# A fused attention and two-layer kernel: GpSimd takes norms, sums of v and low halves for all units, and the opening has a new order

## The chip, the core and the metric

The kernel runs on one core of a Trainium2 chip. The metric is the device time of one execution in microseconds. Five engines work side by side: TensorE (PE; its weight loads, PEld, overlap its products), VectorE (DVE), ScalarE (ACT), GpSimd (POOL) and SyncE (SP), which here only issues DMAs.

## The reference

Three stages follow each other. Attention on q, k, v of 4 x 8 heads, 576 positions and 64 columns is a sum of two parts: one over means of four neighbouring positions, repeated four times, and one local, over the positions at a distance below 4. Then come two feed-forward layers, the first without a nonlinearity other than a product.

```python
q_d, k_d, v_d = (means over 4 positions)
out_up = np.repeat(sm_attn(q_d, k_d, v_d), 4, axis=2)
scores = np.where(np.abs(pos[:, None] - pos[None, :]) < 4, scale * q @ k.T, -1e9)
x = out_up + softmax(scores) @ v                  # (2304, 512)
x = ((x @ w1) * (x @ w2)) @ w3 @ w_out            # d_ff 1024
h = x @ w_in; return (h * sigmoid(h)) @ w_out2    # d_ff 2048
```

## The kernel before

The heads are worked in 16 units of two heads (unit u is batch u // 4, pair u % 4). The two matrices w3 and w_out of the first layer are multiplied with each other once (64 products of weights, a PSUM bank of 128x512 each), so that one product is left behind a * b. All inputs are 64-bit floats; a weight arrives as pairs of 32-bit words, and four steps turn them into a 32-bit float: a scale on ScalarE (L210) and shift, clamp and join on VectorE (L221, L215, L227). Operands of the large products are split into a high half (ScalarE) and a low half (a subtraction), and three passes are summed.

The program has an opening, a middle and an end. The opening is written out by hand: `OPENING` is a list of step names, and every engine runs the steps that concern it in the order of that list, so the list sets the order on TensorE, VectorE, ScalarE, GpSimd and the DMA queue of SyncE at once. An engine that waits for one step holds up all of its later ones. After the list the same kinds of steps for units 7 to 15 are placed between products by a table of due times.

Names in the list, with the unit's number at the end: `Lq`, `Lr`, `Lva`, `Lvb` load q and k, v in groups of four, and v in windows; `pq` sums q and k over four positions (VectorE); `s` and `sd` are the scores, local and coarse; `mk`, `ml`, `md` mask and maxima; `x0` to `x2` and `xd` the exponentials with their sums; `rl` and `rd` inverses of the sums; **`n0` to `n2` and `nd` the norms** (exponentials times inverse); `tl0` to `tl2`, `td0`, `td1` transposes of the result on TensorE, `cl`, `cd` their copies out of PSUM; **`pv0`, `pv1` the sums of v**; `od`, `ol` the products with v; `os`, `xf` the sum x, `xh` its high half, **`xo` its low half**. `L` with `wt`, `wo`, `ww12_` loads a weight, `a`, `d2`, `d1`, `d3` are the four decode steps (scale, shift, clamp, join), `h`, `l` the halves of a w12 piece. `p` with half, group and number is one product of weights; `z0`, `z1` are wide products on zeros that only keep TensorE at work, as the nine at the very start do. `ab`, `af`, `cf`, `Sc` are products with w1 and w2, copy, product a * b and store; the first twelve groups of them stand in the list.

Before the change a unit's number decides on the engine: for units 0 to 4 the norms are twelve ScalarE instructions, and `pv` and `xo` run on VectorE; from unit 5 on all three run on GpSimd, a norm as one instruction over all blocks, issued by the step `n0` (`n1`, `n2` do nothing then). `Ed` is the tile of coarse exponentials, `band` that of local ones, `vr` and `vd` those of v.

Of the kernel before, what the change touches and what calls it, by code (L numbers as in the profile page):

```python
# [11 lines left out]
ALU = mybir.AluOpType  # L12
# [6 lines left out]
NQB, QW, KW = 9, 32, 38  # L19
# [27 lines left out]

OPENING = """
Lwt000 Lwt001 Lwt002 Lq0 Lwo00 Lwo01 Lwt010 Lwt011 at00a d2t00a Lwo10 d1t00a Lwo11 at00b d3t00a
d2t00b d1t00b d3t00b Lva0 at00c d2t00c d1t00c d3t00c Lvb0 s0 pq0 Lr0 ao0a d2o0a sd0 z0 z1 mk0 ml0  # L50
Lq1 ao0b d1o0a d3o0a x00 md0 p000 Lwo20 x10 d1o0b p001 d2o0b xd0 d3o0b Lq2 p002 d2t01 x20 p003 rd0
Lwo21 at01 rl0 p004 p005 nd0 d1t01 Lwt020 p006 d3t01 Lwt021 n00 Lwo30 td00 n10 d2o1 td10 Lwo31 p007
n20 pv00 ao1 pv10 Lwt030 pq1 s1 cd00 cd10 tl00 tl10 d1o1 Lr1 cl00 sd1 cl10 d3o1 tl20 od0 Lwt031 cl20
md1 p010 os0 xd1 pq2 p011 Lq3 ao2 p012 d2o2 Lwt100 p013 rd1 mk1 nd1 p014 d1o2 Lwt101 d3o2 sd2 at02
d2t02 s2 Lww12_00 md2 p015 d1t02 p016 Lww12_01 d3t02 ao3 p017 ml1 ol0 Lq4 d1o3 x01 Lwt110 p020 pv01
x11 pv11 p021 d2o3 Lva1 x21 d3o3 p022 at03 p023 rl1 Lr2 d2t03 p024 n01 d1t03 n11 p025 d3t03 Lvb1 n21
p026 pq3 p027 Lwt111 p030 d2t10 at10 xf00 p031 Lww12_20 xf10 xh00 td01 d1t10 xh10 td11 cd01 d3t10
Lww12_21 p032 cd11 xd2 tl01 d2w12_0 tl11 p033 xo00 cl01 rd2 cl11 tl21 xo10 aw12_0 p034 mk2 ml2 od1
cl21 wh00 d1w12_0 p035 nd2 p036 os1 wh01 d3w12_0 p037 x02 ol1 wh02 wh03 pv02 p100 x12 Lva2 Lvb2 p101
x22 xf01 p102 xf11 hw12_0 rl2 td02 pv12 td12 n02 d2t11 Lr3 p103 n12 lw12_0 p104 n22 d2w12_2 sd3 xh01  # L60
xh11 xo01 cd02 s3 xo11 cd12 md3 tl02 at11 Lq5 tl12 pq4 p105 cl02 p106 cl12 aw12_2 d1t11 tl22 d3t11
od2 cl22 xd3 p107 os2 Lwt120 d1w12_2 p110 Lwt121 d3w12_2 sd4 rd3 ol2 Lww12_30 hw12_2 mk3 Lww12_31
ml3 nd3 p111 lw12_2 Lva3 Lvb3 x03 p112 xf02 p113 x13 xf12 pv03 td03 x23 d2t12 td13 p114 pv13 at12
md4 Lr4 p115 rl3 xh02 d1t12 s4 xh12 n03 d3t12 p116 Lq6 n13 p117 xo02 Lwt130 n23 xo12 Lwt131 p120
d2w12_3 cd03 cd13 pq5 p121 xd4 tl03 tl13 pv04 aw12_3 p122 rd4 p123 cl03 d1w12_3 cl13 nd4 tl23
d3w12_3 od3 p124 cl23 os3 Lww12_10 hw12_3 mk4 p125 Lww12_11 ml4 at13 p126 lw12_3 p127 x04 d1t13 ol3
x14 d2t13 d3t13 x24 sd5 Lva4 Lvb4 pv14 s5 Lww12_50 rl4 Lr5 xf03 aw12_1 p131 md5 pq6 xh03 Lww12_51
p130 p134 p133 n14 xo03 p135 p137 wh10 xf13 td04 td14 n04 Lq7 ab000a d2w12_1 cd04 cd14 p132 d1w12_1
tl04 xd5 n24 d3w12_1 od4 ab000b s6 ab000c p136 cl04 os4 tl14 wh11 wh13 ab001a ab001b Lr6 tl24 af00
wh12 ab001c ab100a Lq8 cl14 d2w12_5 mk5 xh13 Lva5 ml5 Lww12_40 ab101a cl24 cf00 ol4 xo13 ab020a  # L70
aw12_5 rd5 pv05 x25 x15 ab021a Lww12_41 xf14 Sc00 Lvb5 ab020b xf04 d1w12_5 ab100b nd5 ab100c x05
af10 td05 ab101b ab101c rl5 hw12_1 td15 d3w12_5 ab020c xh04 cf10 ab030a ab030b Lva6 cd15 Lww12_60
ab021b n05 ab021c n15 n25 cd05 pv15 tl05 lw12_1 xo04 tl15 af02 cl05 ab030c af03 ab031a ab031b ab031c
cl15 Lr7 sd6 Sc10 pv06 hw12_5 ab120a tl25 cf02 d2w12_4 Sc02 Lww12_61 cf03 md6 aw12_4 Sc03 xd6 ab121a
ab110a pq7 ab120b cl25 xh14 ab121b ab130a ab130b mk6 od5 pv16 s7 ab110b ab110c ml6 x26 os5 pv07 x06
ab120c d1w12_4 ab121c ol5 d3w12_4 af12 ab130c ab111a Lq9 af11 rd6 x16 cf12 af13 hw12_4 ab111b xo14
nd6 ab011a lw12_5 ab111c ab010a xf05 ab010b ab011b aw12_6 rl6 ab131a ab010c cf11 n06 td06 xf15 Lr9
ab131b n16 n26 tl06 af01 Lww12_70 Lww12_71 cd06 Lva8 ab050a cl06 Sc12 xh15 tl16 d2w12_6 ab011c
lw12_4 Lvb8 d1w12_6 cf01 tl26 mk7 ml7 ab131c cf13 ab050b cl16 td16 cl26 sd7 xh05 ab150a cd16 xo05
od6 ab150b ab150c aw12_7 ab050c Lvb6 ab051a ab051b md7 ab051c ab151a xd7 pq8 ab151b x17 pv17 af15  # L80
rd7 Sc11 af05 os6 d2w12_7 d3w12_6 cf05 Lr8 ol6 x07 xf16 xo15 x27 Sc01 Sc13 nd7 ab040a xh16 ab151c
xf06 cf15 rl7 hw12_6 Sc05 Lva7 ab040b Lvb7 ab040c ab140a d1w12_7 ab141a Sc15 xo16 ab140b d3w12_7
ab041a ab140c xh06 ab141b lw12_6 af04 n17 ab141c ab041b af14 ab041c cf14 cf04 Sc04 hw12_7 lw12_7 n07
Sc14 xo06 n27
""".split()


# [1 line left out]
def tile_model(ctx: ExitStack, tc: tile.TileContext, qk, vw, vr, w12, w3t, wo, wb, out):  # L89
    nc = tc.nc  # L90
    wide = wo.dtype != F32

    def pool(stack, name, side, space=None, bufs=1):
        kw = {} if space is None else {"space": space}
        return stack.enter_context(
            tc.tile_pool(name=name, bufs=bufs, side=side, reuse_waits="tile", **kw)
        )
# [59 lines left out]
    for c in range(2):  # L157
        nc.gpsimd.tensor_tensor(
            out=even[:, GW * c:GW * c + GW], in0=zero[:, :GW], in1=zero[:, :GW], op=ALU.subtract
# [9 lines left out]
    for g in range(4):  # L169
        mv = mask[QW * g:QW * g + QW]  # L170
        nc.gpsimd.affine_select(
            out=mv, in_=mv, compare_op=ALU.is_ge, fill=NEG, base=0,
# [3 lines left out]
            out=mv, in_=mv, compare_op=ALU.is_ge, fill=NEG, base=6,  # L176
# [140 lines left out]
    A = {}  # L317
    opening = [True]

    def side(u):  # L320
        return nc.vector if u < 5 else nc.gpsimd

    def load_qk(u):
        t = att.tile([P, 1158], F32, tag="qk", name=f"qk{u}")
        nc.sync.dma_start(t, qk[u // 4, u % 4])
        A["qk", u] = t
# [27 lines left out]
    def unit_ops(u):  # L354
# [18 lines left out]
            nc.vector.reciprocal(out=sv, in_=sv)  # L373

        def norm(z, E, n, width, lo, hi):
            if u < 5:
                for j in range(lo, hi):
                    nc.scalar.mul(E[:, j, :], E[:, j, :], z[:, NQB + j:NQB + j + 1])
            elif lo == 0:
                nc.gpsimd.tensor_tensor(  # L380
                    out=E, in0=E, op=ALU.mult,
                    in1=z[:, NQB:NQB + n].unsqueeze(2).to_broadcast([P, n, width]),
                )
# [120 lines left out]

        def pool_v0():
            r = A["vr", u][:HD]
            side(u).tensor_tensor(
                out=r[:, :, 0:2, :], in0=r[:, :, 0:2, :], in1=r[:, :, 2:4, :], op=ALU.add
            )

        def pool_v1():
            r = A.pop(("vr", u))[:HD]
            t = att.tile([HD, 2, P], F32, tag="vd", name=f"vd{u}", bufs=1)
            side(u).tensor_tensor(out=t, in0=r[:, :, 0, :], in1=r[:, :, 1, :], op=ALU.add)
            hold["vd"] = t

        def coarse_sums():
# [48 lines left out]
        def x_parts(h):  # L566
            for c0, n, g, i0 in PIECES[u // 4][h]:
                if (g, u % 4) not in X:
                    X[g, u % 4] = xpool.tile(
                        [P, 2, GW], F32R, tag=f"x{g % 5}", name=f"x{g}_{u % 4}", bufs=4  # L570
                    )
                    if (g, u % 4) == (3, 0):
                        gap(xpool, 64, "gap_x")
                x = X[g, u % 4][:, :, 64 * i0:64 * (i0 + n)]
                yield x, hold["xf", h][:, 64 * c0:64 * (c0 + n)]
# [4 lines left out]

        def x_rest(h):
            for x, xf in x_parts(h):
                side(u).tensor_tensor(
                    out=x[:, 1], in0=xf, in1=x[:, 0].bitcast(F32), op=ALU.subtract
                )

# [2 lines left out]
        op("xd" + U, coarse_exps)  # L589
        op("rd" + U, lambda: inverse(hold["zd"], 3, 0.25))  # L590
        op("nd" + U, lambda: norm(hold["zd"], hold["Ed"], 3, SD, 0, 3))
        op("s" + U, local_scores)
        op("mk" + U, local_mask)
        op("ml" + U, local_max)
        for k in range(3):
            op(f"x{k}" + U, lambda k=k: exps(hold["zl"], [EL[:, j, :] for j in range(NQB)], EL, range(3 * k, 3 * k + 3), 1.0))
            op(f"n{k}" + U, lambda k=k: norm(hold["zl"], EL, NQB, KW, 3 * k, 3 * k + 3))
            op(f"tl{k}" + U, lambda k=k: local_turn(k))
            op(f"cl{k}" + U, lambda k=k: local_copy(k))
        op("rl" + U, lambda: inverse(hold["zl"], NQB, 1.0))  # L600
        for h in range(2):
            op(f"td{h}" + U, lambda h=h: coarse_turn(h))
            op(f"cd{h}" + U, lambda h=h: coarse_copy(h))
            op(f"xf{h}" + U, lambda h=h: x_sum(h))
            op(f"xh{h}" + U, lambda h=h: x_high(h))
            op(f"xo{h}" + U, lambda h=h: x_rest(h))
        op("pv0" + U, pool_v0)
        op("pv1" + U, pool_v1)
        op("od" + U, coarse_sums)
        op("os" + U, coarse_out)  # L610
# [829 lines left out]
    E = mybir.EngineType  # L1440
    with tc.manual_schedule(engines={E.PE, E.DVE, E.Activation, E.Pool, E.SP}):
        for t in range(NT):
# [10 lines left out]
            for i in range(7):  # L1453
                j = 7 * t + i
# [18 lines left out]
        for u in range(NUN):  # L1473
            t, p = divmod(u, 8)
# [98 lines left out]
```

## Time and profile before

| | us |
|---|---|
| median of 3 runs | 794.08 |
| the runs | 793.44, 794.08, 799.55 |
| the profiled execution | 792.25 |
| its span, first to last instruction | 790.5 |
| TensorE busy | 781.7 |
| VectorE busy | 574.1 |
| ScalarE busy | 448.2 |
| GpSimd busy | 79.5 |

[...] A row of a timeline gives start, duration, engine, line, operation, written and read tiles and shapes, and in brackets how long the engine stood idle before it and what ended that. Durations of neighbours overlap a little; the start of the next row is the better end.

### The profile page before, as it was taken

Reading aid. Unit: us, or ns where it says so; the run is one execution under the profiler, and the core shown is the slowest. Engines: PE = TensorE matmul, PEld = TensorE weight load, DVE = VectorE, ACT = ScalarE, POOL = GpSimd, SP = SyncE. Lnnn points to the kernel's source line nnn. Section 1 sums busy time; section 2 is a strip of 40 time slices with the busy share of each in tenths; the row PEclk is TensorE's granted clock in tenths of the full one; section 3 lists DMA queues with packets and bytes.
Section 4 is the critical chain, followed back from the end, with each engine's and each line's share of the span. In section 5 each row is a group of like instructions: output and inputs, shape, how many; then the busy total and the mean of one; then the engine's idle time right before and its main releaser. Section 6 shows DMA issues by size and latency. Waiting matters only on the chain.

```text
span 790.5 us, 19444 instructions
## 1 busy us (share of the span) xinstructions
PE 781.7 (99%) x7706; PEld 729.6 (92%) x7706; DVE 574.1 (73%) x883; ACT 448.2 (57%) x1148; POOL 79.5 (10%) x99
## 2 busy tenths in 40 slices
PE   8899999999999999999999999999999999999998
PEld 5455699999999999999999999999999999999998
DVE  7888699679878764847889567445665898777771
ACT  6688777554565541525447568556587745444441
POOL 3000045433334210000000000000000000000000
PEclk9999999999999999999999999999999999999999
DMA  9987766779888788525485654463797955666540
GB/s 304 357 253 240 236 205 193 234 222 287 290 289 288 261 270 268 159 54 194 135 314 155 215 177 114 113 196 96 226 280 226 344 198 191 199 198 192 195 139 27
DMA packets 108138, 168.69 MB, mean 213 GB/s; under 512 B 16912, under 2 KB 78864, under 8 KB 107664
## 3 DMA queue, kind: packets, MB, share of 16 engines
q1 hardware_dynamic: 108048, 167.46, 65.8%
q8 instruction: 60, 0.98, 0.5%
q14 instruction: 30, 0.25, 0.1%
HBM read 115.00 MB, written 52.43 MB: 212 GB/s over the span
## 4 chain that ended last, share of the span: by engine, by line
PE 96%; DMA 2%; DVE 0%; SPq 0%; issue 0%; ACT 0%
PE ab L704 26%; PE yb L1161 11%; PE ox L1354 10%; PE hx L1215 9%; PE wp L665 6%; PE hy L1215 6%; PE oy L1354 6%; PE hv L1215 3%; PE hz L1215 3%; PE oz L1354 3%; PE ov L1354 3%; PE ol L545 3%; DMA qk<-qk 1%; PE s L438 1%; PE td L463 1%; PE od L523 1%
## 5 line engine op out<-in xcount | busy, mean ns | idle before, releaser
L704 PE MATMUL ab<-x,w_wB 128*128 128x256 f32 x864 | 109.2, 282 | 0.0
L704 PE MATMUL ab<-x,w_wA 128*128 128x256 f32 x864 | 107.6, 281 | 0.0
L704 PEld LDWEIGHTS ab<-x,w_wB 128*128 128x128 f32 x864 | 102.4, 188 | 1.9 <-issue 1.3
L704 PEld LDWEIGHTS ab<-x,w_wA 128*128 128x128 f32 x864 | 101.6, 188 | 2.0 <-issue 1.5
L1161 PE MATMUL yb<-co,wy 128*128 128x384 f32 x504 | 87.5, 336 | 0.0
L1161 PEld LDWEIGHTS yb<-co,wy 128*128 128x128 f32 x504 | 87.3, 188 | 0.0
L1215 PE MATMUL hx<-yc,wc 128*128 128x384 f32 x432 | 82.9, 336 | 0.0
L1215 PEld LDWEIGHTS hx<-yc,wc 128*128 128x128 f32 x432 | 75.7, 188 | 0.0
L715 ACT COPY af<-ab 128x256 f32<-128x256 f32 x72 | 26.4, 371 | 67.4 <-PE ab L704 60.5
L665 PE MATMUL wp<-w_wo,w_w 128*128 128x512 f32 x128 | 59.5, 601 | 0.1
L1215 PE MATMUL hy<-yc,wc 128*128 128x384 f32 x288 | 57.7, 336 | 0.0
L1354 PE MATMUL oy<-wo,S 128*128 128x256 f32 x432 | 51.9, 276 | 0.0
L1354 PE MATMUL ox<-wo,S 128*128 128x256 f32 x432 | 51.9, 276 | 0.0
L1197 ACT ACTIVATE c<-c 128x384 f32<-128x384 f32 x96 | 48.0, 525 | 4.9 <-DVE c L1127 4.2
L1215 PEld LDWEIGHTS hy<-yc,wc 128*128 128x128 f32 x288 | 50.6, 188 | 0.0
L1354 PEld LDWEIGHTS ox<-wo,S 128*128 128x128 f32 x432 | 50.3, 188 | 0.0
L1354 PEld LDWEIGHTS oy<-wo,S 128*128 128x128 f32 x432 | 50.3, 188 | 0.0
L363 ACT ACTIVATE band<-band,sml 128x38 f32<-128x38 f32 x144 | 44.9, 316 | 5.2 <-DVE sml L454 5.2
L720 DVE TENSOR_TENSOR cf<-ab,af 128x256 f32<-128x256 f32 x72 | 29.9, 416 | 22.6 <-PE ab L704 12.2
L665 PEld LDWEIGHTS wp<-w_wo,w_w 128*128 128x128 f32 x128 | 22.6, 190 | 22.0 <-issue 20.2
L1221 ACT COPY p<-hx 128x384 f32<-128x384 f32 x24 | 11.5, 480 | 43.2 <-PE hx L1215 43.2
L1026 ACT CAST co<-cb 128x768 fp32r<-128x768 f32 x32 | 25.7, 836 | 17.1 <-DVE cb L1010 13.7
(188 smaller groups left out, 1463.4 us busy)
## 6 DMA issues: line engine op xcount, KB each, us to landing
gd<-c SPq DMA_DIRECT2D x96, 192.0 KB
sw<-wb SPq DMA_DIRECT2D x32, 512.0 KB
qk<-qk SPq DMA_DIRECT2D x16, 579.0 KB
big<-gd SPq DMA_DIRECT2D x18, 512.0 KB
A<-gd SPq DMA_DIRECT2D x18, 512.0 KB
S<-gd SPq DMA_DIRECT2D x17, 512.0 KB
cb<-cd SPq DMA_DIRECT2D x10, 768.0 KB
st<-w SPq DMA_DIRECT2D x14, 512.0 KB
```

The lines of the kernel that those rows point to most:

```text
L363: nc.scalar.activation(E[:, j, :], src[j], AF.Exp, bias=z[:, j:j + 1], scale=scale, accum_out=z[:, NQB + j:NQB + j + 1],)
L545: nc.tensor.matmul(acc[h][r, c0:c0 + QW], lhsT=v[k, sub, c, r], rhs=ET[k, c, q0:q0 + QW], start=True, stop=True,)
L665: nc.tensor.matmul(wp_ps[half, j], lhsT=w3v[:, k, j * P:(j + 1) * P], rhs=wov[:, k, :], start=(gp == 0 and k == 0), stop=(gp == 3 and k == 1),
L704: nc.tensor.matmul(acc[:, :GW], lhsT=wv[:, i, w, kk, :], rhs=X[g, kk][:, j, :], start=(n == 0), stop=(n == 11),)
L715: mark(nc.scalar.copy(af, C.pop(("ab", g, m, 0))[:, :GW]))
L720: nc.vector.tensor_tensor(out=cf, in0=C.pop(("ab", g, m, 1))[:, :GW], in1=C.pop(("af", g, m)), op=ALU.mult)
L1026: nc.scalar.copy(d[:, 0], src)
L1161: nc.tensor.matmul(acc[e], lhsT=WY[o][:, a, 2 * g + k, c0:c0 + P], rhs=y[:, b, k, :], start=(n < 2 and (a, b) == (0, 0) and i in (0, 1, 2, ...
L1197: nc.scalar.activation(v, v, AF.Silu)
L1215: nc.tensor.matmul(acc, lhsT=WC[s][:, a, c, kt * P:(kt + 1) * P], rhs=y[:, b, kt, :], start=(n == 0 and i in (0, 1, 2, 4)), stop=(n == 5), ...
L1221: nc.scalar.copy(p1, X_)
L1354: nc.tensor.matmul(acc, lhsT=A[:, a, p * P:(p + 1) * P], rhs=B_[name, p // 4][:, b, p % 4, :], start=(p == 0 and q == 0 and name in begin) ...
```

## The change

`side(u)` and the branch for units below 5 go away: norms, `pv` and `xo` run on GpSimd for every unit. The list of the opening has the same step names in a new order from its 27th step on.

```diff
-    def side(u):
-        return nc.vector if u < 5 else nc.gpsimd
-
...
         def norm(z, E, n, width, lo, hi):
-            if u < 5:
-                for j in range(lo, hi):
-                    nc.scalar.mul(E[:, j, :], E[:, j, :], z[:, NQB + j:NQB + j + 1])
-            elif lo == 0:
+            if lo == 0:
                 nc.gpsimd.tensor_tensor(
...
         def pool_v0():
             r = A["vr", u][:HD]
-            side(u).tensor_tensor(
+            nc.gpsimd.tensor_tensor(
...
-            side(u).tensor_tensor(out=t, in0=r[:, :, 0, :], in1=r[:, :, 1, :], op=ALU.add)
+            nc.gpsimd.tensor_tensor(out=t, in0=r[:, :, 0, :], in1=r[:, :, 1, :], op=ALU.add)
...
         def x_rest(h):
             for x, xf in x_parts(h):
-                side(u).tensor_tensor(
+                nc.gpsimd.tensor_tensor(
...
-d2t00b d1t00b d3t00b Lva0 at00c d2t00c d1t00c d3t00c Lvb0 s0 pq0 Lr0 ao0a d2o0a sd0 z0 z1 mk0 ml0
+d2t00b d1t00b d3t00b Lva0 at00c d2t00c d1t00c d3t00c Lvb0 s0 pq0 z0 ao0a d2o0a z1 Lq1 d1o0a d3o0a
```

Where the instructions stand, first on TensorE, from the first scores to the second ones (spare are the wide products, wp the products of weights with their bank's number). Before:

```order
L438 MATMUL s0_190<-qk0_163 32x38 x36
L409 MATMUL sd0_234<-qkd0_227 64x144 x6
L164 MATMUL spare_115<-even_116 128x512 x6
L665 MATMUL wp0_0_261<-w_wo_231,w_w3_171 128x512
...
L463 MATMUL td0_0_311<-ident_104,Ed0_272 72x128 x3
L463 MATMUL td0_1_319<-ident_104,Ed0_272 72x128 x3
L665 MATMUL wp0_3_285<-w_wo_231,w_w3_171 128x512
L438 MATMUL s1_336<-qk1_250 32x38 x36
L493 MATMUL tl0_0_378<-ident_104,band_111 102x128 x2
```

And now:

```order
L432 MATMUL s0_190<-qk0_163 32x38 x36
L164 MATMUL spare_115<-even_116 128x512 x6
L403 MATMUL sd0_251<-qkd0_227 64x144 x6
L659 MATMUL wp0_2_259<-w_wo_232,w_w3_171 128x512
...
L457 MATMUL td0_0_302<-ident_104,Ed0_269 72x128 x3
L659 MATMUL wp0_0_274<-w_wo_232,w_w3_171 128x512
L487 MATMUL tl0_0_313<-ident_104,band_111 102x128 x2
L457 MATMUL td0_1_318<-ident_104,Ed0_269 72x128 x3
L487 MATMUL tl0_2_327<-ident_104,band_111 102x128 x2
L487 MATMUL tl0_4_330<-ident_104,band_111 38x128
L659 MATMUL wp0_3_261<-w_wo_232,w_w3_244 128x512
L432 MATMUL s1_336<-qk1_238 32x38 x36
```

The wide products moved ahead of sd0; all eight products of the first group of weights, all transposes of unit 0 and one product of the second group now stand ahead of s1.

On VectorE behind the sums of the first q and k (lent and w_wo are the words and the result of w_out's decode, L215 the clamp, L227 the join). Before:

```order
L345 TENSOR_REDUCE qkd0_227<-qk0_163 128x288
L221 TENSOR_SCALAR lent_165<-lent_165 128x512
L448 SCALAR_TENSOR_TENSOR band_111<-s0_190,mask_110 128x9x38
L454 TENSOR_REDUCE sml_248<-band_111 128x9
L215 TENSOR_SCALAR w_wo_231<-w_wo_231 128x512
L227 SCALAR_TENSOR_TENSOR w_wo_231<-w_wo_231,lent_165 128x512
```

And now:

```order
L342 TENSOR_REDUCE qkd0_227<-qk0_163 128x288
L221 TENSOR_SCALAR lent_165<-lent_165 128x512
L215 TENSOR_SCALAR w_wo_232<-w_wo_232 128x512
L227 SCALAR_TENSOR_TENSOR w_wo_232<-w_wo_232,lent_165 128x512
L442 SCALAR_TENSOR_TENSOR band_111<-s0_190,mask_110 128x9x38
L215 TENSOR_SCALAR w_wo_232<-w_wo_232 128x512
```

The join of the first half of w_out moved ahead of mask and maximum.

On GpSimd, which before had nothing between the masks and unit 6's sums of v, the new rows begin so:

```order
L181 MEMSET mask_110 32x3
L374 TENSOR_TENSOR Ed0_269<-Ed0_269,smd_263 128x432
L374 TENSOR_TENSOR band_111<-band_111,sml_249 128x9x38
L501 TENSOR_TENSOR vr0_276<-vr0_276 72x2x256
L508 TENSOR_TENSOR vd0_334<-vr0_276 72x256
L374 TENSOR_TENSOR Ed1_415<-Ed1_415,smd_407 128x432
```

The two norms of a unit and its sums of v take turns there. In the queue of loads the second q and k and the third pair of w3 moved ahead of vr0:

```order
L329 DMA vw0_183<-vw 40x2x512
L322 DMA qk1_238<-qk 128x1158
L257 DMA st_246<-w3t 128x1024 x2
L335 DMA vr0_276<-vr 80x1024
L257 DMA st_285<-wo 128x1024 x2
L322 DMA qk2_382<-qk 128x1158
```

Before, vr0 stood directly behind the windows of v, then the second q and k, a piece of w_out and the third q and k.

## Rows read from the trace of the kernel before

**Rows 1.** The page: busy us (share of the span) and count of each engine.

```profile
PE 781.7 (99%) x7706; PEld 729.6 (92%) x7706; DVE 574.1 (73%) x883; ACT 448.2 (57%) x1148; POOL 79.5 (10%) x99
```

**Rows 2.** Whom TensorE waited for: us in total, times, longest.

```profile
PE s L438 <- DMA qk<-qk: 2.6, 2, 2.0
PE sd L409 <- DVE qkd L345: 1.4, 1, 1.4
```

**Rows 3.** TensorE's timeline: start, us, operation, count of passes, idle before.

```profile
8.33 0.85 PE L438 MATMUL s<-qk 64*32 64x38 f32 x72 [0.61 <-DMA qk<-qk]
...
11.48 1.66 PE L164 MATMUL spare<-even 128*128 128x512 f32 x6
12.98 6.26 PE L665 MATMUL wp<-w_wo,w_w 128*128 128x512 f32 x14
...
22.75 0.85 PE L438 MATMUL s<-qk 64*32 64x38 f32 x72 [1.99 <-DMA qk<-qk]
23.53 0.64 PE L493 MATMUL tl<-ident,band 128*102 128x128 f32 x4
...
86.33 5.42 PE L665 MATMUL wp<-w_wo,w_w 128*128 128x512 f32 x12
```

**Rows 4.** The DMA queue's timeline: start and us of the issues.

```profile
13.48 0.33 SPq L325 DMA_DIRECT2D qk<-qk  x1
...
20.57 1.31 SPq L257 DMA_DIRECT2D lent<-wo  x2
22.72 0.33 SPq L257 DMA_DIRECT2D lent<-w3t  x1
...
28.01 1.59 SPq L257 DMA_DIRECT2D lent<-w3t  x2
```

**Rows 5.** VectorE's timeline.

```profile
9.20 1.35 DVE L345 TENSOR_REDUCE qkd<-qk 128x288 f32<-128x1152 f32 x1
...
12.22 0.69 DVE L227 SCALAR_TENSOR_TENSOR w_wo<-w_wo,lent 128x512 int32<-128x512 int32 x1
...
17.70 1.23 DVE L227 SCALAR_TENSOR_TENSOR w_w<-w_w,lent 128x1024 int32<-128x1024 int32 x1
18.84 0.69 DVE L221 TENSOR_SCALAR lent<-lent 128x1024 int32<-128x1024 int32 x1
...
104.79 1.17 DVE L227 SCALAR_TENSOR_TENSOR dec<-dec,st 128x1024 int32<-128x1024 int32 x1
```

**Rows 6.** ScalarE's timeline: the first of twelve exponentials, and the scale behind them.

```profile
11.95 0.33 ACT L363 ACTIVATE band<-band,sml 128x38 f32<-128x38 f32 x1 [0.42 <-DVE sml L454]
...
15.82 1.12 ACT L210 ACTIVATE w_w<-lent 128x1024 f32<-128x1024 f32 x1
```

**Rows 7.** GpSimd's groups: count, busy us, mean ns, idle before.

```profile
L507 POOL TENSOR_TENSOR vr<-vr 72x512 f32<-72x512 f32 x11 | 16.1, 1468 | 90.7 <-DMA vr<-vr 90.7
L583 POOL TENSOR_TENSOR x<-xf,x 128x256 fp32r<-128x256 f32 x15 | 13.0, 879 | 0.4 <-ACT x L579 0.4
L380 POOL TENSOR_TENSOR Ed<-Ed,smd 128x432 f32<-128x432 f32 x11 | 10.7, 974 | 38.5 <-DVE smd L373 21.7 <-ACT af L715 7.4 <-ACT dec L210 4.3
L514 POOL TENSOR_TENSOR vd<-vr 72x256 f32<-72x256 f32 x11 | 9.8, 890 | 33.3 <-PE od L523 33.3
L380 POOL TENSOR_TENSOR band<-band,sml 128x342 f32<-128x342 f32 x11 | 9.5, 866 | 26.2 <-DVE sml L373 26.2
```

**Rows 8.** VectorE's groups of joins within the first 180 us.

```profile
L227 DVE SCALAR_TENSOR_TENSOR dec<-dec,st 128x1024 int32<-128x1024 int32 x7 | 9.9, 1418 | 0.2
...
L227 DVE SCALAR_TENSOR_TENSOR dec<-dec,sw 128x1024 int32<-128x1024 int32 x3 | 3.6, 1217 | 0.0
```

**Rows 9.** GpSimd's timeline: a local norm.

```profile
105.05 1.54 POOL L380 TENSOR_TENSOR band<-band,sml 128x342 f32<-128x342 f32 x1 [1.59 <-DVE sml L373]
```

**Rows 10.** Busy us of each engine in two stretches, granted clock, DMA share.

```profile
0.00:80.00 80.00, 74.63 (x841) 41.52 (x842) 67.21 (x124) 59.38 (x215) 7.76 (x22) 1.00 0.88 288
80.00:180.00 100.00, 100.00 (x1505) 87.69 (x1506) 78.23 (x145) 64.12 (x247) 34.53 (x35) 1.00 0.70 219
```

## What this leads one to expect of the change

> **What bounds the kernel now.** I read the page's busy line first: TensorE is busy for 781.7 of 790.5 us, VectorE for 574.1, ScalarE for 448.2, GpSimd for 79.5 [rows 1]. So time can only come out of TensorE's waits, and a faster helper engine is worth what TensorE waits for it. Next, all of TensorE's waits: beside the start there are two lines, 2.6 us in two waits for q and k, of which the longer is 2.0, and 1.4 us for VectorE's reduction [rows 2]. TensorE's timeline says where they lie; the reader is to look at the brackets. 0.61 us stand ahead of s0, 1.99 us ahead of s1 at 22.75 [rows 3], and the 1.4 between them ahead of sd0. After 23 us the list has none. Third, what stands behind the waits: SyncE's issues, of which each waits for the landing of the transfer eight places earlier, so that their starts tell when those landed [rows 4], and VectorE's and ScalarE's rows [rows 5, 6]. Last, GpSimd's prices [rows 7] and what it does to VectorE [rows 8 to 10].
>
> Most that can be won: 1.4 + 2.0 = **3.4 us**. The 0.61 us stays, since the first twelve loads are the same.
>
> **The change, part by part.** Durations are of one execution of 792.25 us (span 790.5, 1.75 around it), 1.83 us below the median of 794.08; the runs lie between 793.44 and 799.55.
>
> *Work moved.* For each of units 0 to 4 ScalarE loses twelve norm instructions and VectorE five additions and subtractions; GpSimd gains the two norms, 0.97 + 0.87, the sums of v, 1.47 + 0.89, and the low halves, 2 x 0.88 + 0.5 (the last an estimate, below the 0.88 of a row four times as wide) [rows 7]: 6.5 us a unit, 32 in all. TensorE's instructions stay the same ones. None of this is on TensorE's path by itself; it is priced through the waits that follow.
>
> *The opening walked through* (from the rows' durations, 0.06 to 0.1 us taken off where one instruction starts before the last has ended):
> - s0 ends at 9.18 as before. The six wide products, 1.66 us, now stand ahead of sd0 and fill the wait for the reduction, which ends at 10.55 [rows 3, 5]. sd0 starts at 10.84 and takes some 0.9.
> - The first product of weights needs the decode of w_out's first half. Behind the reduction VectorE now runs its three steps in a row (the last 0.69), without mask and maximum between them: done at 11.95, where it was 12.91 [rows 5]. The product starts at 12.0, not 12.98. Wait 0.25.
> - Four products of 0.87 (seven, in fourteen passes, take 6.1 us [rows 3]) reach 15.5; the next needs the second half, done at about 15.6 after mask, maxima and one early shift. Wait 0.15.
> - Three products reach 18.2, then td0 needs the norm. ScalarE's decode of the second w3 pair now stands ahead of the exponentials and can't start before its load landed at 13.48 [rows 4]; 1.12 for it, 0.32 for each exponential (twelve take 3.87 us) [rows 6]: sums ready at 16.6, inverse 16.95, GpSimd's norm 17.95. No wait, or up to 0.9 if VectorE's next 1.23 us step holds the norm up.
> - tl0 needs the second norm: exponentials 18.45, inverse 18.85, norm 19.75, against 19.5 on TensorE. Wait 0.25. The rest of td and tl shares two PSUM banks with ScalarE's copies: 0.3. The product behind them needs the next w_out pair: ScalarE 19.57, two more steps on VectorE, 21.45. Wait 0.3.
> - s1 at 22.4. The second q and k no longer stand behind vr0 (320 KB): the loads of v before it had landed at 20.57, vr0 and it by 22.72 (899 KB in 2.15 us), so it now lands near 21.9 [rows 4]. What was 1.99 is gone.
> - vr0 itself now lands behind q and k and two pieces of w3, at about 1.3 us each (four landings from 22.72 to 28.01 [rows 4]): near 25.4. GpSimd sums v by 28.4 at the latest; od0 is reached at about 29.3. Hidden, with 0.9 us to spare. s2's load comes 2.9 MB after s1's, near 29.3, and is asked for at 30.8.
>
> New waits: 0.25 + 0.15 + 0.25 + 0.3 + 0.3 = 1.25, say 1.5 with the switches between kinds of product, of which the new order has about a dozen more. At s1 TensorE is 0.35 us earlier and has one product (0.87) and all of tl0 (0.65 [rows 3]) more behind it: a lead of **1.9 us**.
>
> *From there to 180 us* the old order has no wait, so the new one can only keep or lose the lead. VectorE has 13 us less to do (pv 1.1 and low halves near 1 for each unit, and what the ends overlap), GpSimd 32 us more. Tightest is the last decode of w3. In the old order its join starts at 83.84 us with about 72 us of VectorE's work behind it (67.2 in the first 80 us [rows 10]); without pv of five units and low halves of three it is 64. TensorE's first product with it started at 86.33 [rows 3]; with one td (0.7) more ahead of it and 1.9 us of lead it is asked for at 85.1. VectorE begins at 4.0 and waits some 4 us for loads up to 30 us: 85.1 - 8 - 64.5 = 12.6 us of margin, which delays by GpSimd have to eat first. The norms of units 0 to 2 have only one product or two between norm and turn; a norm held up takes 1.54, not 0.87 [rows 9], so two of them are charged, 0.7 together after what the products hide.
>
> Sum: -3.4 + 1.5 + 0.7 = -1.2; I take **-1.1 us**: 791.15 us in the profile's terms, **793.0 us** against the median.
>
> **A rule against the change.** At 104.79 us a join on VectorE begins, 1.17 us; GpSimd's norm, started at 105.05, takes 1.54 us and ends 0.6 after the join [rows 5, 9]. So they seem to exclude each other there. [...] How much it adds, rows say: ten full joins (seven at 1418 ns, three at 1217 [rows 8]; 1.23 us with GpSimd at rest [rows 5]), of which two ran before GpSimd began at 93 us; the other eight take 9.9 + 3.6 - 2.5 = 11.0 us in place of 9.8, 12% more, with GpSimd busy for 34.5 of 100 us [rows 10]. In the new opening GpSimd would be busy for 27 of 79 us up to that last decode, the same share. [...]
>
> **Rivals.**
> - *All of it comes back.* The norms arrive in time everywhere and the waits of the walk shrink to 0.3: -3.1, 791.0 us. For it: VectorE and ScalarE have the shorter queues. Against it: the walk has four places without slack. 0.2.
> - *GpSimd holds VectorE up and the last decodes come late.* The place is the product that needs the last w3 decode. [...] With every microsecond of GpSimd added (27 us) it is +12.5, 806.6. [...] Against it: those eight joins. 0.17.
> - *The loads.* w3's third pair and vr0 land at the pace of 13.48 to 20.57 (1.38 MB in 7.1 us) in place of 1.3 us for 512 KB: vr0 at 30.4, the decode five us later, about 4 us of new waits at od0 and the next products, +2.5: 796.6 us. Against it: the four landings after 22.72; the slow pace has a load over 40 partitions in it. 0.06.
> - *Nothing moves.* The new waits equal the old ones: 794.1 us. 0.07.
>
> **How the numbers follow.** The forecast has 0.5: a gain of 0.2 to 2 us, 792.1 to 793.9. Range: from 790.5 (all back, and the scatter of the runs) to 797.0, which takes in the loads' case and the first part of GpSimd's; beyond it lies its worse half. A measurement of this kernel tells about 1%, 7.9 us, from no change. More than that can't be won: the waits hold 3.4. To lose it takes a delay of 0.55 per us: 0.04. So 0.01 faster, 0.95 the same, 0.04 slower.
>
> **What would show it.** In TensorE's rows: the wide products ahead of sd0; the first product of weights near 12.0; td0 near 18.2; no wait of 2 us at s1, and s1 near 22.4; od0 near 29.3. GpSimd busy for about 112 us; VectorE's 574 down by 13, less what longer joins give back. Wrong would be: a mean of the joins above 1.6 us before 85 us, a wait of TensorE for VectorE's join or for GpSimd of over a microsecond, or s2 waiting for its load.

## The result and the profile after

The changed kernel takes 803.00 us (median of 11 runs, 796.00 to 804.91), the kernel before 794.74 beside it: ratio **1.0077, 95% from 1.0048 to 1.0106**. Forecast were 793.0 and a range up to 797.0. The profiled execution took 799.39 us, span 797.6, 7.1 more than before.

In one of the traces below the last stage's passes take 281 ns, in all others 276, which makes 6 us of the span, nearly as much as the 8 by which the runs of the kernel before scatter (793.44 to 801.33); traces are therefore compared at the first product of yb, ahead of that stage: **353.13 us before, 358.97 after**, 5.84 later.

The page of the changed kernel answers [rows 1]: busy us, share, count.

```profile
PE 785.8 (99%) x7706; PEld 729.5 (91%) x7706; DVE 570.1 (71%) x858; ACT 434.4 (54%) x1088; POOL 114.4 (14%) x134
```

All waits of its TensorE, the answer to [rows 2]: us in total, times, longest.

```profile
PE ol L539 <- issue: 1.7, 1, 1.7
PE spare L152 <- DVE zero L148: 1.3, 1, 1.3
PE ol L539 <- DMA vw<-vw: 1.0, 1, 1.0
PE ab L698 <- issue: 1.0, 1, 1.0
PE td L457 <- POOL Ed L374: 0.7, 1, 0.7
PE s L432 <- DMA qk<-qk: 0.6, 1, 0.6
PE hx L1209 <- ACT u L1223: 0.6, 1, 0.6
PE wp L659 <- DVE w_wo L227: 0.6, 2, 0.3
PE sd L403 <- DVE qkd L342: 0.3, 1, 0.3
```

The two waits that were to go are gone (the 1.4 ahead of sd0 and the 2.0 for q and k at s1). In their place stand three of over 1 us that the prediction had no term for: one for a load of v, and two put down to "issue", which no semaphore ends. TensorE's timeline, which answers [rows 3], shows where they fall: the number in brackets is the wait ahead of the row. A row counts passes; here a product of float32 operands is two passes, each with its own weight load (the 36 products of s1 are 72 passes, and the page has 7706 passes and 7706 loads).

```profile
19.09 0.52 PE L457 MATMUL td<-ident,Ed 128*72 128x128 f32 x3 [0.68 <-POOL Ed L374]
...
23.41 0.85 PE L432 MATMUL s<-qk 64*32 64x38 f32 x72
...
30.62 0.71 PE L517 MATMUL od<-EdT,vd 72*64 72x144 f32 x8
...
33.10 1.35 PE L539 MATMUL ol<-ET,vw 38*64 38x32 f32 x72
...
54.21 1.25 PE L539 MATMUL ol<-ET,vw 38*64 38x32 f32 x68 [1.03 <-DMA vw<-vw]
55.39 4.54 PE L659 MATMUL wp<-w_wo,w_w 128*128 128x512 f32 x6
...
80.68 0.85 PE L432 MATMUL s<-qk 64*32 64x38 f32 x72
81.46 0.71 PE L517 MATMUL od<-EdT,vd 72*64 72x144 f32 x8
82.10 1.13 PE L659 MATMUL wp<-w_wo,w_w 128*128 128x512 f32 x2
83.16 0.95 PE L403 MATMUL sd<-qkd 64*64 64x144 f32 x12
84.04 1.12 PE L659 MATMUL wp<-w_wo,w_w 128*128 128x512 f32 x2
85.10 1.01 PE L539 MATMUL ol<-ET,vw 38*64 38x32 f32 x54
87.85 0.55 PE L539 MATMUL ol<-ET,vw 38*64 38x32 f32 x18 [1.74 <-issue]
88.33 2.84 PE L659 MATMUL wp<-w_wo,w_w 128*128 128x512 f32 x6
...
156.87 1.35 PE L539 MATMUL ol<-ET,vw 38*64 38x32 f32 x72
158.16 1.42 PE L698 MATMUL ab<-x,w_wA 128*128 128x256 f32 x10
160.61 2.45 PE L698 MATMUL ab<-x,w_wA 128*128 128x256 f32 x20 [1.03 <-issue]
```

Two things are to be read here. The wait in ol3 stands between its 54th and 55th of 72 passes, in the middle of one step, where no operand changes. And six weight passes take 4.54 us at 55.39 but 2.84 at 88.33: behind the 1.03 us wait for v the granted clock fell from 1.00 of full to 0.50. By stretches of 1 us (length, busy us of PE, PEld, DVE, ACT, POOL; then clock, DMA share, GB/s):

```profile
57.00:58.00 1.00, 1.00 (x2) 0.34 (x1) 0.10 (x1) 0.00 (x0) 0.76 (x1) 0.50 0.95 232
58.00:59.00 1.00, 1.00 (x3) 0.34 (x1) 0.21 (x1) 0.22 (x1) 0.01 (x1) 0.50 1.05 384
```

The trace's clock record has 0.50 for 3.41 us, from 56.25 us on, and the six passes took 1.7 us longer. Over the span the mean granted clock is 0.997, where it was 1.000 before.

What ends an "issue" wait is in the DMA view, where a queue q8 of the kind "instruction" stands. Whole execution first (packets, MB, share), then the stretch 85.0 to 86.7 us:

```profile
q8 instruction: 60, 0.98, 0.5%
```

```profile
q8 instruction: 1, 0.02, 4.8%
```

The 60 packets are 16 KB each, and TensorE has 7706 passes, as many weight loads and 90 control instructions: about 258 for a packet. Between the waits in ol3 and in ab the trace counts 1014 passes, 1014 loads and 20 control instructions, **2048 = 8 x 256**, and eight packets of q8 begin to come between the two waits. One packet ran from 85.2 to 86.5 us, and ol3 went on at 87.85; another ran from 158.2 to 159.3, and ab went on at 160.61. Counted so, each of the 60 packets begins to come between 38 instructions before and 237 behind the place at which the packet ahead of it comes into use: one is in use and one is on its way, so that one must last until the next has landed.

In the kernel before, the corresponding packet ran from 80.8 to 82.0 us, ahead of the run of small products that starts at 83.50; no wait follows:

```profile
83.50 1.29 PE L545 MATMUL ol<-ET,vw 38*64 38x32 f32 x69
...
85.55 0.85 PE L438 MATMUL s<-qk 64*32 64x38 f32 x72
```

### The profile page after: what moved, and what is told of

The parts are those of the page before. It is cut to its first block, busy times and chain, and to the rows that moved or that the text cites. A ratio compares the mean times of both kernels' runs of the same rounds, so it can differ in the third digit from the quotient of the medians.

```text
span 797.6 us, 19420 instructions
## 1 busy us (share of the span) xinstructions
PE 785.8 (99%) x7706; PEld 729.5 (91%) x7706; DVE 570.1 (71%) x858; ACT 434.4 (54%) x1088; POOL 114.4 (14%) x134
## 4 chain that ended last, share of the span: by engine, by line
PE 91%; DMA 7%; issue 1%; SPq 1%; ACT 0%; DVE 0%; DVEq 0%; ACTq 0%
PE ab L698 26%; PE yb L1155 11%; PE ox L1348 10%; PE hx L1209 9%; PE oy L1348 6%; PE hy L1209 6%; PE wp L659 4%; PE oz L1348 3%; PE hv L1209 3%; PE hz L1209 3%; PE ov L1348 3%; PE ol L539 2%; DMA vw<-vw 2%; DMA lent<-wo 2%; DMA vr<-vr 2%; PE s L432 1%
## 5 line engine op out<-in xcount | busy, mean ns | idle before, releaser
L659 PE MATMUL wp<-w_wo,w_w 128*128 128x512 f32 x128 | 63.3, 622 | 0.6 <-DVE w_wo L227 0.6
L577 POOL TENSOR_TENSOR x<-xf,x 128x256 fp32r<-128x256 f32 (+3 forms) x48 | 39.2, 838 | 17.9 <-ACT x L573 17.8
```

The lines of the kernel that those rows point to most:

```text
L577: nc.gpsimd.tensor_tensor(out=x[:, 1], in0=xf, in1=x[:, 0].bitcast(F32), op=ALU.subtract)
L659: nc.tensor.matmul(wp_ps[half, j], lhsT=w3v[:, k, j * P:(j + 1) * P], rhs=wov[:, k, :], start=(gp == 0 and k == 0), stop=(gp == 3 and k == 1),
```

## The experiments

Theory A (later F): the new order's loads, and packets of instructions used up too fast, cost the time. Theory B: GpSimd and VectorE hold each other up. In the table "issue" are TensorE's waits without a semaphore in the profiled execution.

| run | ratio to before (95%) | first yb, us | issue waits, us |
|---|---|---|---|
| before | 1 | 353.13 | none |
| changed | 1.0077 (1.0048 to 1.0106) | 358.97 | ol3 1.74, ab 1.03 |
| after_again | 1.0030 (0.9997 to 1.0063) | 357.96 | ol3 1.50, ab 0.57, ol 0.21 |
| gp_only | 0.9976 (0.9944 to 1.0009) | 352.11 | 0.23 |
| order_only | 1.0154 (1.0096 to 1.0213) | 364.81 | ol3 1.83, ab 0.89 |
| loads_early | 1.0069 (1.0031 to 1.0106) | 356.92 | ol3 0.48, ab 1.13 |
| after_shift | 0.9999 (0.9970 to 1.0028) | 354.21 | ol4 0.51 |
| before_bad | 1.0011 (0.9979 to 1.0044) | 357.61 | spare 0.99, s4 1.90 |
| fixed | 1.0035 (0.9998 to 1.0072) | 356.16 | 0.28 |
| best_try | 1.0038 (1.0002 to 1.0073) | 355.78 | 0.49 |
| phase_back | 1.0087 (1.0054 to 1.0120) | 362.26 | spare 1.19, ol3 1.44, ab 1.15, ol 1.13 |
| before_shift | 1.0012 (0.9979 to 1.0046) | 353.15 | none |
| loads_late | 1.0095 (1.0063 to 1.0127) | 358.27 | ol3 0.45, ab 0.94 |
| gp_shift | 1.0008 (0.9980 to 1.0037) | 353.79 | none |
| ends_64 | 1.0023 (0.9990 to 1.0056) | 353.82 | 0.26 |
| ends_128 | 1.0001 (0.9971 to 1.0032) | 353.00 | none |
| ends_256 | 1.0081 (1.0049 to 1.0112) | 362.66 | ol3 2.02, ab 0.84 |

The 24 issue waits of the table, in 13 traces, have one thing in common: counted from TensorE's first instruction, every one stands 193 instructions behind a multiple of 256, and ahead of every one a packet of q8 has landed 1.2 to 1.6 us earlier.

### The parts of the change apart

**gp_only**, the engines' part alone:

```diff
 (changed kernel)
-OPENING = the new order
+OPENING = the order of the kernel before
```

> The old opening order with the norms, the sums of v and the low halves of units 0 to 4 on GpSimd. Theory A (the new order's loads and its bunched small products cost the time, the engine move nothing): 794 to 797 us, ratio to the kernel before 0.999 to 1.003; the product ol1 waits under 0.2 us for its window load and the clock stays at full level from 40 to 100 us. Theory B (GpSimd and VectorE hold each other up, decodes and norms come late): ratio 1.005 to 1.011, most of what the whole change lost; VectorE's joins before 85 us average over 1.6 us and TensorE waits over 1 us in sum for VectorE or GpSimd.

0.9976, a little under what theory A said: theory B falls. GpSimd is busy for 118.0 us here and nothing is lost; TensorE's longest wait is the 1.62 us ahead of sd0, which the kernel before has too (1.42).

**order_only**, the other part:

```diff
 (kernel before)
-OPENING = its own order
+OPENING = the new order
```

> The new opening order with the norms on ScalarE and the sums of v and low halves of units 0 to 4 on VectorE, as before the change. Theory A: ratio 1.005 to 1.011, as the whole change, with a wait of about 1 us of ol1 for its window load near 53 us and a stretch at half clock behind it. Theory B: ratio 0.997 to 1.002, since the engines that hold each other up are parted again; if the old engines can't keep the new order's pace, TensorE waits for ScalarE's norms or VectorE's sums and the ratio is above 1.011.

1.0154, more than the whole change, as the last clause had it: ScalarE's norms come late (td0 waits 1.79, tl 0.95) and decodes too (wp 2.4 in three waits), and two stretches of 6.83 us ran at a granted clock of 0.50 (its mean is 0.57 from 22 to 30 us and from 90 to 98 us), one behind td0's wait and one behind ol3's. So the new order needs the other engines. Its wait in ol3 stands at the same place of the stream as in the changed kernel, though neither engine nor load is timed alike:

```profile
91.23 0.86 PE L543 MATMUL ol<-ET,vw 38*64 38x32 f32 x17 [1.83 <-issue]
```

**after_again**, no edit:

> The changed kernel again, beside the others on one chip. Both theories: ratio 1.005 to 1.011 to the kernel before. If the wait of ol1, the stretch at half clock near 57 us and the two waits of over 1 us that no semaphore explains (near 87 and 160 us) belong to the program, they stand in this trace at the same places; if they are accidents of one execution, they are gone or elsewhere.

The ratio, 1.0030, is less than the 1.005 to 1.011 expected, and its interval takes in 1: two measurements of one kernel put the loss at 0.8% and at 0.3%. The wait in ol3 is back after the same 54 passes, and that in ab; the wait for v and the half clock behind it are not, so these were an accident of one execution. The granted clock fell to 0.50 behind ol3 instead, for 3.41 us:

```profile
82.77 1.01 PE L539 MATMUL ol<-ET,vw 38*64 38x32 f32 x54
85.28 0.55 PE L539 MATMUL ol<-ET,vw 38*64 38x32 f32 x18 [1.50 <-issue]
```

**loads_early**:

```diff
-Lr1 ao3 Lww12_20 Lww12_21 ...
+Lr1 Lva1 Lvb1 ao3 Lww12_20 Lww12_21 ...
```

(and Lvb2, Lvb3 right behind Lva2, Lva3)

> The changed kernel with the two window loads of unit 1 put right behind the load Lr1, some 40 steps earlier in the list, and Lvb2 and Lvb3 each right behind Lva2 and Lva3; nothing else. Theory A: no wait of ol1, no fall of the clock behind it: 2.5 to 3.5 us less than the changed kernel (wait 1.0, six passes at half clock 1.9), ratio 1.003 to 1.005. If the fall of the clock has another cause than that wait, it stays and only 1.0 us comes back (ratio 1.0065). Theory B: no change against the changed kernel, ratio 1.0077 plus or minus 0.002.

The wait for v did not appear, but 2.5 to 3.5 us did not come back: 1.0069. Other waits came (td 1.05 for GpSimd's norm, od 0.74 for ScalarE). The wait in ol3 fell to 0.48, that in ab stayed. That the loads of v were the main cause is refuted.

### Where a packet ends

The next runs leave every order and move only the place of TensorE's instructions in their stream, by tiny products at the start, where TensorE idles for the first load. **after_shift** (32 products of four instructions each, less the four of an idle one: 124 places):

```diff
-NWARM = 9
+NWARM = 8
     for _ in range(NWARM):
         idle_product()
+    for _ in range(32):
+        nc.tensor.matmul(
+            spare[:32, :38], lhsT=zero[:64, :32], rhs=zero[:64, :38], start=True, stop=True
+        )
```

> The changed kernel with 32 tiny idle products (32 of 38 columns each) in place of one of the nine idle products that run while the first load is awaited. No order of work changes; every later instruction of TensorE stands 124 places further on in its stream. Theory F (instruction fetch: TensorE's stream comes in packets of 256 instructions, one ahead, and a packet of tiny products is used up before the next has landed): the waits without a semaphore inside ol3 (1.5 to 1.7 us) and inside the ab product near 160 us (0.6 to 1.0) are gone or under 0.3 in sum, and none over 0.5 comes elsewhere before 200 us; first yb product 2 to 3 us earlier than in the changed kernel (355 to 356 us where the two traces had 358.0 and 359.0); ratio to the kernel before 1.000 to 1.004. Rival D (ol3 waits for data or a port, whatever its place in the stream): both waits stay at the same products, ratio 1.003 to 1.008.

Rival D falls: ol3 and ab wait no more, the ratio is 0.9999, the first yb some 4 us earlier, a little better than expected; ol4 has a wait of 0.51 instead.

```profile
82.01 1.35 PE L543 MATMUL ol<-ET,vw 38*64 38x32 f32 x72
83.30 2.84 PE L663 MATMUL wp<-w_wo,w_w 128*128 128x512 f32 x6
```

**before_bad** puts the ends where they hurt in the kernel before (60 tiny products, NWARM 7):

> The kernel before with 60 tiny idle products in place of two of the nine idle ones: every later instruction of TensorE stands 232 places further on, which puts the end of a packet of 256 behind the run ol3, sd4, s4 of tiny products near 84 to 87 us and its start inside that run. Theory F: a wait without a semaphore of 1 to 3 us appears inside s4 near 86 us, and one of 0 to 1 us near 130 us of the kernel's time; first yb product 1.5 to 3.5 us later than in the kernel before (353.1), ratio 1.001 to 1.005. Rival D: no such wait, ratio 0.998 to 1.002.

The wait came inside s4 as counted, and the granted clock fell to 0.50 behind it for 3.41 us:

```profile
86.27 0.75 PE L442 MATMUL s<-qk 64*32 64x38 f32 x61
88.91 0.45 PE L442 MATMUL s<-qk 64*32 64x38 f32 x11 [1.90 <-issue]
89.30 5.21 PE L669 MATMUL wp<-w_wo,w_w 128*128 128x512 f32 x8
```

The first yb is 4.48 us late, more than expected; 0.7 of it was there before (ol3 began at 84.22, not 83.50). The ratio, 1.0011, can't be told from 1. So the wait is shown, what it costs over many executions is not.

**phase_back** (66 tiny products, NWARM 7, so one whole packet) and **before_shift** (the 32 on the kernel before) are the controls:

> The changed kernel with 66 tiny idle products in place of two of the nine idle ones, so that every later instruction of TensorE stands 256 places further on: one whole packet, the packets' ends where they were in the changed kernel. Theory F (instruction fetch): the wait without a semaphore is back inside ol3 after its 54th of 72 products (0.5 to 1.8 us), and the one in the ab product near 160 us (0.5 to 1.1); the start may lose up to 1 us to a fetch among the tiny products, as the run that spoiled the kernel before did (0.99 us); first yb product at 357 to 360 us, ratio 1.003 to 1.009. Rival G (the 32 tiny products helped in another way, by a warmer TensorE or a later start): no such waits, first yb product at 354 to 355.5, ratio 0.998 to 1.002.

> The kernel before with the same 32 tiny idle products for one idle product as in the run that mended the changed kernel. Theory F: the kernel before had no such wait to lose, so nothing changes: ratio 0.998 to 1.002, first yb product 352 to 354.5 us. Rival G: it gains as the changed kernel did, ratio 0.995 to 0.998.

before_shift changed nothing, so rival G falls. In phase_back the wait is back behind the 54th pass, and that of ab:

```profile
83.71 1.01 PE L543 MATMUL ol<-ET,vw 38*64 38x32 f32 x54
86.16 0.78 PE L543 MATMUL ol<-ET,vw 38*64 38x32 f32 x18 [1.44 <-issue]
...
160.79 2.45 PE L702 MATMUL ab<-x,w_wA 128*128 128x256 f32 x20 [1.15 <-issue]
```

Its time is no clean measure of those waits: the tiny products took 4.72 us, an issue wait of 1.19 followed, and sd0 came at 14.70 instead of 10.72. Three more kernels moved the ends with a start meant to be as early as the changed kernel's (18, 35, 71 tiny products with NWARM 7, 6, 2).

> The changed kernel with 35 tiny products for three of the nine idle ones: 128 places further on, first s product at 8.0 to 8.8 us. Theory F: no wait without a semaphore over 0.6 us; what is left of the change is the start that the prediction walked and its small waits: first yb product 352.5 to 354.5 us, ratio 0.997 to 1.002, about 4 us (0.5%) under the changed kernel.

> The changed kernel with 71 tiny products for seven of the nine idle ones: 256 places further on, so that packets end where they do in the changed kernel, one packet later; first s product at 8.0 to 9 us, and up to 1.2 us lost to a fetch near 10 us. Theory F: the waits in ol3 after its 54th product (0.5 to 1.8 us) and near 160 us (0.5 to 1.2 us) are back; first yb product at 357 to 359.5 us, ratio 1.003 to 1.008.

> The changed kernel with 18 tiny products for two of the nine idle ones: every later instruction of TensorE 64 places further on, the first s product as early as before (8.0 to 8.8 us). Counted from the trace of the changed kernel, packets then end 6 to 30 products ahead of ol3's end no more but in the weight products before sd4 and before ol3, behind the first few ab products after ol4 (near 104 us) and behind the first few after ol7 (near 157 us). Theory F: no wait without a semaphore in ol3; one of 0.5 to 2.5 us in the ab product right behind ol4; one of 0.5 to 1.5 us in that right behind ol7; ratio 1.002 to 1.008. Rival (the wait belongs to ol3 itself): 1.5 to 1.7 us in ol3 after its 54th product again.

**ends_128** is the clean one: all its TensorE waits are

```profile
PE spare L152 <- DVE zero L148: 1.3, 1, 1.3
PE sd L407 <- DVE qkd L346: 0.8, 2, 0.4
PE wp L663 <- DVE w_wo L231: 0.2, 1, 0.2
```

and its ol3 runs through, in the same order of the same work:

```profile
82.43 1.35 PE L543 MATMUL ol<-ET,vw 38*64 38x32 f32 x72
83.71 2.84 PE L663 MATMUL wp<-w_wo,w_w 128*128 128x512 f32 x6
```

Its first yb comes at 353.00 us, 0.13 ahead of the kernel before, though s0 began at 9.31, half a microsecond later than meant. **ends_256** has the wait behind the 54th pass again (2.02), but its start was late as well (s0 at 12.39; the record of a granted clock of 1.00 begins only at 16.43 us, against 5.05 in the changed kernel, and the six wide passes behind s0 took 2.86 us against 1.67). Its ol3 began 3.2 us behind that of ends_128 (85.59 against 82.43), so of its 1.0081 some 3 us belong to the start.

**ends_64** was half a miss: ol3 waits no more, as expected, but of the two waits expected behind ol4 and ol7 none came in that execution. The packet that comes into use inside ol4 had begun to come 0.7 us before the one ahead of it was in use, and landed 1.4 us ahead of need, though the one ahead was used up in 1.7 us; a packet that is used up fast is not enough, the fetch of the next has to be late too.

### What makes the fetch late

**loads_late**, four loads behind Lww12_51; TensorE's stream as in the changed kernel:

```diff
-... Lva4 ... Lq6 ... Lvb4 ... Lr6 ... Lww12_50 Lww12_51 ...
+... Lww12_50 Lww12_51 Lva4 Lq6 Lvb4 Lr6 ...
```

> The changed kernel with four loads (Lva4, Lq6, Lvb4, Lr6: 1.26 MB) put behind Lww12_51, which cannot go out before some 88 us; TensorE's stream and its packets unchanged. In the changed kernel seven loads went out between 79.1 and 83.1 us, and the fetch of the packet that ol3 waited for ran from 85.2 to 86.5 us. Theory F with contention (the fetch stands behind loads in the DMA engines): the fetch runs at 82.5 to 84.5 us and the wait in ol3 falls from 1.5 to 1.7 us to under 0.5; the wait near 160 us stays (0.6 to 1.1); ratio 1.001 to 1.006. If the fetch is late for another cause than loads, ol3 waits 1.3 to 1.8 us as before, ratio 1.003 to 1.008. The four late loads may cost a wait of s6 or ol4 of their own.

The fetch ran from 83.0 to 84.0 us and the wait fell as expected, that of ab stayed:

```profile
83.89 1.01 PE L537 MATMUL ol<-ET,vw 38*64 38x32 f32 x54
85.34 0.54 PE L537 MATMUL ol<-ET,vw 38*64 38x32 f32 x18 [0.45 <-issue]
...
101.62 0.38 PE L696 MATMUL ab<-x,w_wB 128*128 128x256 f32 x1 [1.33 <-POOL x L575]
```

The late loads cost a new wait for GpSimd (1.33), and the ratio is no better. But loads_early waited only 0.48 there too, with the same seven loads going out from 78.8 to 82.3 us. So the run doesn't settle what makes a fetch late: that loads in flight do fits it and is not shown, and how the DMA engines order the two was not seen. Over the first 200 us of all 17 traces the two do go together: where loads held the DMA engines for over 90% of the two microseconds around the time at which a packet came into use, the next began to come 2.1 us after it (median of 174), where they held under 30%, 0.5 us after it (46). But these are different places of the program.

### Versions meant to win

**fixed** is loads_early with the 32 tiny products; **best_try** is gp_only with them and `Lq1` ahead of `Lr0`; **gp_shift** is gp_only with them alone.

> Both remedies on the changed kernel: the window loads of units 1 to 3 early as in the run before, and the 32 tiny idle products. Theory F: what stays is TensorE's waits for norms and sums of GpSimd near 18 and 52 us and for ScalarE near 48 us, some 2 us; first yb product at 354 to 356 us, ratio 0.998 to 1.003. Rival D: first yb product at 357, ratio 1.003 to 1.008.

> The old order with the norms, sums and low halves of all units on GpSimd, the load of unit 1's q and k one step earlier (ahead of the first vr), and the 32 tiny idle products. The engine move alone gave 0.9976 (0.9944 to 1.0009). Theory: TensorE's wait for that load near 22 us (2.0 us in the kernel before) is gone, no wait without a semaphore appears; first yb product at 351 to 352 us, ratio 0.995 to 0.999. If vr of unit 0 comes too late in its place, the first od or ol waits 0.5 to 1 us and the ratio is 0.998 to 1.002.

> The old order, the norms, sums and low halves on GpSimd, and the 32 tiny idle products; without the earlier load of q and k that made the first od wait 2.12 us for the sum of v in the last attempt. The engine move alone gave 0.9976 (0.9944 to 1.0009) and a first yb product at 352.1 us, with one fetch wait of 0.2 us. Theory F: no wait without a semaphore over 0.3 us; first yb product 351 to 353 us; ratio 0.996 to 1.000.

None came out as fast as expected. fixed kept its waits for norms (td 1.41 near 52 us) and has 1.0035. best_try fell into the trap that its expectation names: with vr0 later, the first od waits 2.12 us for GpSimd's sum of v, and 3.41 us at a granted clock of 0.50 follow. gp_shift has no issue wait, as said, but equals the kernel before. No version is shown to beat it; the best, gp_only at 0.9976, has an interval that takes in 1.

```profile
25.32 0.73 PE L519 MATMUL od<-EdT,vd 72*64 72x144 f32 x8 [2.12 <-POOL vd L510]
```

## Why the prediction was wrong

- **The walk to od0 held, with half its lead.** sd0 came at 10.72 (10.84 said), the first weight product at 12.00 (12.0), td0 at 19.09 (18.2 to 19.1), s1 at 23.41 (22.4), od0 at 30.62 (29.3), and s2 did not wait. ol0 began at 33.10 where it was 34.92, but sd2 (0.88 us), which stood ahead of it in the old order, was still to come: the lead is 0.9, not 1.9. Most of what is missing is the wait of 0.68 ahead of td0, the "up to 0.9" that was named and not taken: GpSimd's norm took 1.70 us beside a join that ran from 17.07 to 18.27.

```profile
17.34 1.70 POOL L374 TENSOR_TENSOR Ed<-Ed,smd 128x432 f32<-128x432 f32 x1 [8.31 <-DVE smd L370]
```

- **The 2.0 us for q and k was one execution's.** With the old order and its list of loads, this wait at s1 was 1.99 in the trace before, but 0.24 in gp_only, 1.67 in gp_shift and 1.07 in before_shift. So part of the 3.4 us to be won was scatter.
- **The step that failed** is "From there to 180 us the old order has no wait, so the new one can only keep or lose the lead", priced by helper engines and by two loads. By it the rest cost 0.7 us. At ol7, which has the same work ahead of it in both, the changed kernel was 4.74 us late (156.87 against 152.13), and the issue wait in ab was still to come: 5.7 us were lost since ol0. Of these, 1.74 was for instructions, 1.03 for v (Lvb1, which the loads' rival did not look at) and 1.7 at a granted clock of 0.50 behind that wait. The last 1.2 belong to the order itself: ends_128, without an issue wait, loses 1.3 between the same two places (a lead of 1.3 at ol0, of 0.03 at ol7), 0.75 of it in two waits for VectorE's reduction. That the instructions come in packets, and that the new order put nearly all of s4, od3, sd4 and 54 passes of ol3 (from 80.9 us on) with only four weight passes between them into one, used up in 5.2 us, stood in no term.
- **The fetch was the decisive term**: ends_128 leaves order and engines as they are and has 1.0001, where the changed kernel had 1.0077 and 1.0030 (the second one's interval overlaps with that of ends_128; the first yb, 353.00 against 358.97 and 357.96, tells them apart). What the prediction did price, then, came out as no change: its forecast, 793.0 against a median of 794.08, is 0.9986, inside the interval of ends_128, so the gain is neither shown nor refuted.
- **GpSimd's rival** fell, though joins grew by more than argued: full joins before 85 us average 1.47 us against 1.22, 20% more where 12% was said (but under the 1.6 named), and there is no wait for the last w3 decode; gp_only is no slower. No run shows the delay of 0.55 per us on which the chance of 0.04 rests; in its place, over the first 180 us, with GpSimd busy for 75.9 us against 42.3, the shifts of st averaged 944 ns against 793, the clamps of dec 1048 against 830, and the sums of q and k 1342 against 1345. GpSimd's busy time was right (114.4, 112 said); VectorE fell by 4.0 us, not 13, since its joins, shifts and clamps took longer: of the three full joins that write dec before 85 us, 1.22 us each before, one took 1.63 and two 2.16 and 2.28. TensorE hid it, as the margin said.
- **Its sign for "wrong"** named a mean of the joins above 1.6 us, waits of over a microsecond for VectorE or GpSimd, and one for s2's load; none of them came, and the time was wrong all the same. A wait for no semaphore was not on the list.

## What to carry to other kernels

Before many tiny products are put close together, count TensorE's instructions (here four for each float32 product) and see where their packets end (after every 256 in these traces): a packet that is used up in 2.5 to 5.3 us, as those ahead of the waits here were, can leave TensorE standing until the next has landed. With the stream unchanged, the two large waits stood at the same places in every trace, of different length. Look for waits that no semaphore ends, in the middle of a step. If one is there, a few idle products at the start move the ends (32 or 35 tiny ones cost next to nothing here, first yb at 353.15 in before_shift and 353.00 in ends_128 against 353.13; 60 and more delayed the start, ol3 by 0.7 us in before_bad, sd0 by 4.0 in phase_back), and tell in one run whether that is the cause.

## What was not expected of the hardware

- From the landing of an instruction packet to the first pass behind the wait took 1.2 to 1.6 us in all 24 waits (1.33 in ol3 of the changed kernel), the packet itself 0.9 to 1.3 us.
- Of 22 waits of TensorE of 1.0 to 2.1 us that began at a granted clock of 1.00, nine were followed by a stretch at 0.50: 3.41 us behind the 1.03 for v, after_again's 1.50, before_bad's 1.90, phase_back's 1.44 and 1.13 and best_try's 2.12, and 6.83 us behind ends_256's 2.02 and order_only's 1.79 and 1.83. None came behind the other 13, among them the 1.74 in ol3, the 1.99 of the kernel before and loads_late's 1.33. Where it comes it costs 1.7 us or more on top of the wait; what decides whether it comes was not found.
- The tiny products of 64 rows and 38 columns took 37 ns a pass at the start (63 in 2.36 us in after_shift, at full granted clock), those of s, of the same shape, 12 ns (72 in 0.85). Why was not looked for.
- In the profiled execution of gp_only the last stage took 178.3 us from its first ox, in all others 171.8 to 172.4, at full granted clock throughout. Its cause was not looked for.

```profile
L1346 PE MATMUL oy<-wo,S 128*128 128x256 f32 x432 | 53.8, 281 | 0.1
```
